# Two scratch rows in turn for VectorE's maxima in a sliding-window attention and GEGLU kernel

## The chip, the core and the metric

The kernel runs on one core of a Trainium2 chip. The metric is the device time of one execution in microseconds; a median of several runs stands for a kernel. A core has five engines that run side by side, each with its own queue of instructions taken in order: TensorE (PE, with a loader for its weights, PEld), VectorE (DVE), ScalarE (ACT), GpSimd (POOL) and SyncE (SP), which here issues most of the transfers. They meet through semaphores: an instruction may wait for a count that another engine, a transfer, or an earlier instruction of its own engine raises.

## The reference

For x of 2048 tokens by 640 features, with xn = layernorm(x):

```python
qkv = xn @ wqkv                          # 32 heads of 20
scores = q @ k.T * 20 ** -0.5            # key in (query - 256, query]
o = softmax(scores) @ v
h = gelu(xn @ w_gate) * (xn @ w_up)      # 1728 wide
out = x + o @ wo + h @ w_down
```

The softmax needs, for each head and query, the largest score in its window of 256 keys, or another value that keeps the exponentials in range.

## The kernel before

The products keep near float32 precision by splitting each operand into a high and a low part. After the layernorm, the main stage is the function `attention`: it goes through 32 units (8 groups of four heads by 4 chunks of 512 queries), each of 14 slots, and writes out by hand the order of TensorE's, ScalarE's, VectorE's, GpSimd's and SyncE's work. A slot can hold maxima, exponentials, the product with the values, and in any case some matmuls of a filler: the projections to q, k and v, and a part of the gate and up products. When the units are done, the rest of the gate and up products and the output products follow, without maxima.

The maxima belong to `max_pair` (L503). One call takes one head from each half of the array's rows and 128 queries. It takes two PSUM banks (`bank("ps_m")`, L510), computes into each of them the scores of 128 queries against 288 keys (L523), and then VectorE reads each bank once (L527): it adds the mask, which is 0 inside the window and −3e38 outside, and takes the maximum along the row. Only that one number per query is of use; it goes to a column of the tile `mx`. The instruction must write the masked sums somewhere too, and that is `junk`, 128 partitions by 288 bfloat16, which nobody reads. In the profile one such maximum is two instructions of VectorE, both on L527: the maximum (`junk<-ps_m,mask`) and the read of its accumulator (`mx<-`).

There are 8 such pairs per unit, pulled from a stream by `pull_max` two at a time: in the slots 0, 4 and 8, and in slot 0 a second time after `av_unit`, the product with the values (L622). So 4 maxima make one burst, and 512 are run in all. When a unit's 16 are done, `negate` (L536, L537) turns them and `max_end` (L541, its matmul is L544) brings them into the rows of the stacked queries, so that the exponential of `exp_piece` (scores L582, ScalarE's exponential L584) already has the maximum subtracted.

All these matmuls write to one ring of six PSUM banks (the pool `psr`, L482): `ps_m`, `ps_o` (two for each product with the values), `ps_e` and `ps_n`. A matmul that starts in a bank waits until the reader of the bank's previous content is done: VectorE for `ps_m`, ScalarE for the others. Which bank of the ring each of them gets isn't written in the kernel: the framework's planner hands out the one that it believes free first. The same planner places every tile and sets every wait. The filler writes to two other banks (`psd`, L132), which VectorE also reads in parts of the projections (L273) and of the gate and up products (L677, L685, L692).

A tile of a pool with `bufs=1` has one place: whoever writes a new tile of that tag waits until all accesses to the old one are over. That holds for an engine's own earlier instructions too: the planner adds a wait on VectorE's own semaphore. Where an instruction needs two waits, the second is an instruction of the engine's sequencer ahead of it (EVENT_SEMAPHORE in the profile, not counted as busy). Here that is the usual case: one wait is for TensorE's scores, one for the maximum before.

Of the kernel before, what the change touches and what calls it, by code (L numbers as in the profile page):

```python
# [11 lines left out]
BF = mybir.dt.bfloat16  # L12
# [58 lines left out]
def block_kernel(ctx, tc, x, wqk, wv, wgu, wdo, wdl, out):  # L71
# [143 lines left out]
    def late(fn, *a):  # L215
        if now[0] is None or now[0] < NS:
            fn(*a)
        else:
            lates.append((fn, a))
# [263 lines left out]
    ap = pr.enter_context(tc.tile_pool(name="ap", bufs=2, side="right", reuse_waits="tile"))  # L483
# [14 lines left out]
    def bank(name):  # L498
        return psr.tile([128, C], F32, name=name, tag="ring")
# [3 lines left out]
    def max_pair(u, i):  # L503
        g, c = divmod(u, NC)
        jj, b = divmod(i, 4)
        q, k = qs[u % NQ], ks[u % NK]
        if i == 0:
            maxes[u] = ap.tile([128, 4, 4], F32, name="mx", tag="mx")
        n = 128 * b + 128 if c == 0 and b < 2 else 288
        pss = [bank("ps_m") for _ in range(2)]  # L510
        todo = []
        for h in range(4):
            q0 = 128 * b + 32 * h
            k0 = q0 + 32 - n
            parts = [(max(0, -k0), n, k, max(0, k0), q0 + 32)]
            if k0 < 0:
                parts.append((0, -k0, ks[(u - 1) % NK], C + k0, C) if c else (0, -k0, k, 0, None))
            todo += [(i_, h, q0, *part) for i_, part in enumerate(sorted(parts, key=lambda p: p[1] - p[0]))]
        for _, h, q0, lo, hi, kt, k0, k1 in sorted(todo, key=lambda p: p[:2]):
            for r, ps in enumerate(pss):  # L520
                rows, j = slice(64 * r, 64 * r + SR), 2 * r + jj
                keys = kt[rows, j, k0:k1] if k1 else kt[rows, j, 0:1].to_broadcast([SR, hi])
                nc.tensor.matmul(ps[32 * h:32 * h + 32, lo:hi], q[rows, j, q0:q0 + 32], keys,  # L523
                                 start=True, stop=True, tile_position=(64 * r, 32 * h))
        junk = ap.tile([128, 288], BF, name="junk", tag="junk", bufs=1)
        for r, ps in enumerate(pss):
            nc.vector.tensor_tensor_reduce(out=junk[:, 0:n], in0=ps[:, 0:n], in1=mask[:, 288 - n:288], scale=1.0,  # L527
                                           scalar=NEG, op0=OP.add, op1=OP.max,
                                           accum_out=maxes[u][:, 2 * r + jj, b:b + 1])
        if i == 7:  # L530
            mx = maxes.pop(u)
            nm = nms[u % 2]
            maxes[u] = nm

            def negate():
                nc.vector.tensor_scalar(nm[:, 0, 0], mx, -1.0, None, op0=OP.mult)  # L536
                nc.vector.scalar_tensor_tensor(nm[:, 0, 1], mx, -1.0, nm[:, 0, 0], op0=OP.mult, op1=OP.subtract)  # L537

            late(negate)
# [262 lines left out]
    def pull_max(n, slot):  # L802
        for _ in range(n):
            x = next(stream, None)
            if x is None:
                return
            max_pair(*x)
            if x[1] == 7:
                at(slot + (MXD if slot >= 0 else 4), max_end, x[0])
# [714 lines left out]
```

## Time and profile before

| | |
|---|---|
| median of 3 runs | 1045.38 us (1043.09 to 1048.82) |
| profiled execution | 1044.52 us |
| its span, first to last instruction | 1042.8 us |
| TensorE busy | 1027.2 us (99%) |
| VectorE busy | 728.3 us (70%) |
| of that the maxima, L527 | 512, 445 ns in the mean, from 62.8 to 540.6 us |
| mean granted clock of TensorE | 0.999 |

The span is what the trace covers; the execution's time has 1.7 us around it. Busy shares are means over stages that differ. Matmuls overlap in the array and their ends are modelled, so TensorE's busy time says that something was under way and not that the array was full: part of a stop can lie under the recorded length of the matmul before it.

### The profile page before, as it was taken

What the parts mean: (1) busy time and instruction counts of PE and PEld (TensorE: products, weight loads), DVE (VectorE), ACT (ScalarE), POOL (GpSimd) and SP (SyncE); (2) the same over time, 40 slices, a digit from 0 to 9 for tenths busy, and PEclk for the clock granted to TensorE, in tenths of its full rate; (3) what the DMA queues carried; (4) which work ended last, traced back from release to release, by engine and by line L of the source; (5) the groups of instructions that cost most, each with busy time, mean ns of one, the idle gap of its engine ahead of it and who ended that gap; (6) DMA issues with size and microseconds to landing.
All of it is one profiled execution on the core that took longest, in us unless ns stands there. A gap on an engine that the chain in (4) does not pass through costs nothing.

```text
span 1042.8 us, 28733 instructions
## 1 busy us (share of the span) xinstructions
PE 1027.2 (99%) x10941; PEld 853.3 (82%) x10941; DVE 728.3 (70%) x2007; ACT 527.8 (51%) x1120; POOL 377.1 (36%) x543
## 2 busy tenths in 40 slices
PE   8999999999999999999999999999999999999998
PEld 7987776677678876777677888888888999999998
DVE  8845666666665566776653778777556879888887
ACT  4444667666666667666666522323234544333332
POOL 5221778876565568665755111110110000000000
PEclk9999999999999999999999999999999999999999
DMA  5652465555333354444332557666216874443342
GB/s 201 190 148 62 134 180 162 171 158 175 104 105 93 94 168 135 150 126 142 100 92 91 190 187 248 232 240 243 102 66 248 257 234 137 136 128 119 119 137 92
DMA packets 105203, 158.95 MB, mean 152 GB/s; under 512 B 15420, under 2 KB 60092, under 8 KB 105064
## 3 DMA queue, kind: packets, MB, share of 16 engines
q1 hardware_dynamic: 102680, 150.95, 45.9%
q10 hardware_dynamic: 2384, 6.16, 1.9%
q8 instruction: 86, 1.41, 0.6%
q14 instruction: 53, 0.43, 0.1%
HBM read 101.78 MB, written 54.92 MB: 150 GB/s over the span
## 4 chain that ended last, share of the span: by engine, by line
PE 84%; DVE 7%; DMA 4%; ACT 2%; issue 1%; SPq 1%; POOL 0%; ACTq 0%; DVEq 0%
PE ps_d L110 22%; PE ps_g L968 21%; PE ps L1235 14%; PE ps_e L582 8%; PE ps_v L110 7%; PE ps_o L622 6%; PE ps_m L523 4%; DVE junk L527 2%; PE ps_g L110 1%; DVE ss L1073 1%; DMA qs<-qd 1%; DVE at L1073 1%; PE ps_t L181 1%; DVE wt L1073 1%; DMA stg<-wtd 1%
## 5 line engine op out<-in xcount | busy, mean ns | idle before, releaser
L527 DVE CUSTOM_DVE_ANT_0 junk<-ps_m,mask 128x288 bf16<-128x288 f32 (+2 forms) x512 | 227.8, 445 | 140.3 <-PE ps_m L523 82.5
L584 ACT ACTIVATE P<-ps_e 128x512 f32<-128x512 f32 (+2 forms) x384 | 195.5, 574 | 60.0 <-PE ps_e L582 58.9
L1235 PE MATMUL ps<-wb,at 128*128 128x320 f32 x999 | 156.4, 310 | 0.8 <-DVE xr L1261 0.7
L1235 PEld LDWEIGHTS ps<-wb,at 128*128 128x128 f32 x999 | 148.9, 188 | 1.4 <-issue 0.9
L595 POOL TENSOR_SCALAR_AFFINE_SELECT P<-P 128x512 f32<-128x512 f32 x128 | 83.8, 656 | 93.5 <-ACT P L584 92.2
L582 PE MATMUL ps_e<-qs,ks 124*128 124x128 bf16 (+2 forms) x704 | 107.3, 277 | 2.1 <-DVE mx L527 2.0
L110 PE MATMUL ps_d<-xh,wql 128*128 128x512 f32 x350 | 105.3, 410 | 0.0
L110 PE MATMUL ps_d<-xl,wqh 128*128 128x512 f32 x350 | 105.3, 410 | 0.0
L110 PE MATMUL ps_d<-xh,wqh 128*128 128x512 f32 x350 | 105.3, 411 | 0.0
L1235 PE MATMUL ps<-wt,at 128*128 128x320 f32 x552 | 89.3, 310 | 0.4 <-DVE u L1073 0.4
L582 PEld LDWEIGHTS <-ks 124*128 124x128 bf16 x704 | 51.5, 98 | 41.0 <-issue 24.0
L1235 PEld LDWEIGHTS ps<-wt,at 128*128 128x128 f32 x552 | 82.9, 188 | 0.9 <-DVE u L1073 0.9
L1189 ACT ACTIVATE at<-ss 128x512 fp32r<-128x512 f32 x59 | 37.3, 633 | 91.4 <-DVE ss L1073 91.4
L622 PE MATMUL ps_o<-P,v 64*32 64x320 f32 (+5 forms) x2816 | 82.0, 348 | 0.0
L103 POOL TENSOR_TENSOR wql<-wr,wqh 128x640 fp32r<-128x640 f32 x11 | 17.6, 1605 | 173.9 <-PE ps_g L968 129.4
L598 POOL TENSOR_SCALAR_AFFINE_SELECT P<-P 128x512 f32<-128x512 f32 x112 | 71.3, 647 | 16.9 <-ACT P L584 16.8
L622 PEld LDWEIGHTS ps_o<-P,v 64*32 64x32 f32 x2816 | 66.7, 106 | 9.8 <-DVE mx L527 4.5
L110 PEld LDWEIGHTS ps_d<-xh,wql 128*128 128x128 f32 x350 | 63.9, 189 | 12.8 <-issue 1.6
L110 PEld LDWEIGHTS ps_d<-xh,wqh 128*128 128x128 f32 x350 | 63.3, 189 | 12.6 <-issue 0.9
L110 PEld LDWEIGHTS ps_d<-xl,wqh 128*128 128x128 f32 x350 | 63.6, 189 | 12.1 <-issue 1.5
L523 PE MATMUL ps_m<-ks,qs 60*32 60x96 bf16 (+5 forms) x3008 | 64.9, 244 | 3.8 <-DVE mx L527 2.3
L259 POOL TENSOR_TENSOR pt<-r,pt 128x512 bf16<-128x512 f32 x40 | 46.8, 1170 | 57.4 <-ACT pt L258 57.4
(196 smaller groups left out, 1889.4 us busy)
## 6 DMA issues: line engine op xcount, KB each, us to landing
hr<-hd SPq DMA_DIRECT2D x104, 128.0 KB
hd<-he SPq DMA_DIRECT2D x50, 256.0 KB
wr<-wgu SPq DMA_DIRECT2D x27, 320.0 KB
qs<-qd SPq DMA_DIRECT2D x64, 120.0 KB
ks<-kd SPq DMA_DIRECT2D x64, 120.0 KB
xi<-x SPq DMA_DIRECT2D x16, 320.0 KB
qs<-qd SPq DMA_DIRECT2D x64, 80.0 KB
ks<-kd SPq DMA_DIRECT2D x64, 80.0 KB
```

What stands on the lines that cost most here:

```text
L110: nc.tensor.matmul(ps, a(k), b(k), start=n == 0, stop=n == 3 * nk - 1)
L259: nc.gpsimd.tensor_tensor(out=pt[:, l, :], in0=r, in1=pt[:, 1, :], op=OP.subtract)
L523: nc.tensor.matmul(ps[32 * h:32 * h + 32, lo:hi], q[rows, j, q0:q0 + 32], keys, start=True, stop=True, tile_position=(64 * r, 32 * h))
L527: nc.vector.tensor_tensor_reduce(out=junk[:, 0:n], in0=ps[:, 0:n], in1=mask[:, 288 - n:288], scale=1.0, scalar=NEG, op0=OP.add, op1=OP.max ...
L582: nc.tensor.matmul(ps[:, col:col + n], k[0:QROWS, j, kc:kc + 128], q[0:QROWS, j, q0:q0 + n], start=True, stop=True)
L584: nc.scalar.activation(pt[:, j, lo:hi], ps[:, lo:hi], AF.Exp, scale=SCALE)
L595: nc.gpsimd.affine_select(out=a, in_=a, pattern=[[0, 4], [1, 128]], compare_op=OP.is_ge, fill=0.0, base=0, channel_multiplier=-1)
L598: nc.gpsimd.affine_select(out=a, in_=a, pattern=[[0, 4], [-1, 128]], compare_op=OP.is_ge, fill=0.0, base=-1, channel_multiplier=1)
L622: nc.tensor.matmul(halves[h][32 * j:32 * j + 32, q0:q0 + n], v[rows, w0_:w0_ + 32], pts[u, bi][rows, j, col:col + n], start=i == 0, stop=i ...
L968: nc.tensor.matmul(ps, i, j, start=first and n == 0, stop=n == len(work) - 1, skip_group_check=True)
L1189: nc.scalar.activation(hi[:, 3:7], s, AF.Copy)
L1235: nc.tensor.matmul(ps[bank][:, 0:HD], *work[bank][j], start=bank not in begun, stop=final[p, bank] == n and j == len(work[bank]) - 1, skip ...
```

## The change

The scratch row is taken inside the loop over the two banks, so that each maximum has a tile of its own, where the two maxima of a pair had one together; and the tag has two places in place of one.

```diff
@@ -522,8 +522,8 @@
                 keys = kt[rows, j, k0:k1] if k1 else kt[rows, j, 0:1].to_broadcast([SR, hi])
                 nc.tensor.matmul(ps[32 * h:32 * h + 32, lo:hi], q[rows, j, q0:q0 + 32], keys,
                                  start=True, stop=True, tile_position=(64 * r, 32 * h))
-        junk = ap.tile([128, 288], BF, name="junk", tag="junk", bufs=1)
         for r, ps in enumerate(pss):
+            junk = ap.tile([128, 288], BF, name="junk", tag="junk", bufs=2)
             nc.vector.tensor_tensor_reduce(out=junk[:, 0:n], in0=ps[:, 0:n], in1=mask[:, 288 - n:288], scale=1.0,
                                            scalar=NEG, op0=OP.add, op1=OP.max,
                                            accum_out=maxes[u][:, 2 * r + jj, b:b + 1])
```

The number of instructions on the engines stays the same in the code; the order written out by hand stays too. The tile takes 576 bytes per partition, once more than before.

## The prediction

> **What bounds the kernel now.** I read the page first: the busy times, then the group of the line that the change touches.
>
> ```profile
> span 1042.8 us, 28733 instructions
> PE 1027.2 (99%) x10941; PEld 853.3 (82%) x10941; DVE 728.3 (70%) x2007; ACT 527.8 (51%) x1120; POOL 377.1 (36%) x543
> L527 DVE CUSTOM_DVE_ANT_0 junk<-ps_m,mask 128x288 bf16<-128x288 f32 (+2 forms) x512 | 227.8, 445 | 140.3 <-PE ps_m L523 82.5
> ```
>
> TensorE (PE) sets the time: of 1042.8 us it is idle 1042.8 − 1027.2 = 15.6. VectorE (DVE) has slack on average, so whatever a faster maximum saves there counts only where TensorE waits for a maximum. The view of the line itself gives where the maxima lie, and that nearly all of them have a wait of their own ahead of them.
>
> ```profile
> L527 DVE CUSTOM_DVE_ANT_0 junk<-ps_m,mask x512: 278/458/460, 62.8 to 540.2; 128x288 bf16<-128x288 f32 x149, 128x128 bf16<-128x128 f32 x11, 128x256 bf16<-128x256 f32 x11
> L527 DVE DVE_READ_ACCUMULATOR2_ANT mx<- x512: 76/83/86, 63.0 to 540.6; 128x1 f32 x171
> ```
>
> ```profile
> L527 DVEq EVENT_SEMAPHORE  x469: 21/21/21, 63.2 to 540.1; - x157
> ```
>
> So only the stretch from 62.8 to 540.6 us, the attention, can change; what follows has no maxima. Each maximum is two instructions: the masked maximum (0.46 us) and the read of its accumulator (0.08 us), and 469 of 512 have a sequencer wait in front. Next come the waits for the maxima, in the stretch from 60 to 560 us: engine and line, who released it, total us, times, longest.
>
> ```profile
> PE ps_m L523 <- DVE mx L527: 2.3, 7, 0.3
> PE ps_e L582 <- DVE mx L527: 2.0, 6, 0.5
> PEld ps_o L622 <- DVE mx L527: 4.5, 9, 0.5
> PEld L544 <- DVE mx L527: 3.2, 12, 0.3
> ```
>
> These four are the whole field of the change: matmuls that need a bank of the six-bank ring which a maximum still reads. The first two are idle time of TensorE itself, 4.3 us; the others are idle time of its weight loader, beside which TensorE may be working. Last, the chain of waits over the same 500 us:
>
> ```profile
> by line: PE ps_d L110 42.2%; PE ps_e L582 16.4%; PE ps_o L622 11.3%; PE ps_v L110 10.5%; PE ps_m L523 8.3%; DVE junk L527 3.4%; DMA qs<-qd 2.5%; issue 1.4%; SPq L494 0.8%; SPq L268 0.5%; ACT P L584 0.5%; PE ps_n L544 0.4%; DVE nm L536 0.3%;
> ```
>
> The maxima hold 3.4% of it, 17 us. That isn't what a faster maximum could give back, since TensorE works beside most of it, but it serves as a check below.
>
> **The change, part by part.** No instruction is removed and none added: 512 maxima, 512 accumulator reads. What moves is the row that the masked sums are written to. Where all write one row, each maximum must wait until the one before it has written; with two rows in turn it needs the one before that. In the program before, 432 of the 512 wait for the maximum directly in front of them. One burst shows what that costs, both engines together:
>
> ```profile
> 181.53 0.81 PE L523 MATMUL ps_m<-ks,qs 60*32 60x288 bf16 x6
> 181.54 0.46 DVE L527 CUSTOM_DVE_ANT_0 junk<-ps_m,mask 128x288 bf16<-128x288 f32 x1
> 181.93 0.08 DVE L527 DVE_READ_ACCUMULATOR2_ANT mx<- 128x1 f32 x1
> ...
> 182.16 0.46 DVE L527 CUSTOM_DVE_ANT_0 junk<-ps_m,mask 128x288 bf16<-128x288 f32 x1
> ...
> 182.54 0.08 DVE L527 DVE_READ_ACCUMULATOR2_ANT mx<- 128x1 f32 x1
> 182.68 0.31 PE L523 MATMUL ps_m<-ks,qs 60*32 60x288 bf16 x7 [0.33 <-DVE mx L527]
> ...
> 182.77 0.46 DVE L527 CUSTOM_DVE_ANT_0 junk<-ps_m,mask 128x288 bf16<-128x288 f32 x1
> ```
>
> The period is 0.61 us (181.54, 182.16, 182.77): the accumulator read starts 0.38 after the maximum, overlapping its end, is done at 0.47, and then nothing runs for 0.14 us until the next maximum starts. An instruction that has nothing to wait for behaves otherwise:
>
> ```profile
> 414.38 0.46 DVE L527 CUSTOM_DVE_ANT_0 junk<-ps_m,mask 128x288 bf16<-128x288 f32 x1
> 414.77 0.09 DVE L527 DVE_READ_ACCUMULATOR2_ANT mx<- 128x1 f32 x1
> 414.77 0.69 DVE L273 TENSOR_TENSOR r<-ps_d,pt 128x512 f32<-128x512 f32 x1
> ```
>
> ```profile
> 175.30 0.69 DVE L273 TENSOR_TENSOR r<-ps_d,pt 128x512 f32<-128x512 f32 x1 [1.62 <-POOL pt L259]
> 175.90 0.45 DVE L527 CUSTOM_DVE_ANT_0 junk<-ps_m,mask 128x288 bf16<-128x288 f32 x1
> ```
>
> The subtraction at 414.77 starts together with the accumulator read, 0.39 after the maximum. The maximum at 175.90 starts 0.09 before the recorded end of the instruction ahead of it; it has its wait for an earlier maximum too, one that was long over, so a wait already met costs nothing. What the trace doesn't show is a maximum straight behind another without the wait. The bounds: 0.47, if it must let the accumulator read finish (gain 0.14 each), and 0.38, if it overlaps as the subtraction does (gain 0.23). A loss has no row: the wait can only be met earlier. I take 0.38, the row nearest in kind, and keep 0.14 for the range.
>
> The Trainium skill, page "VectorE: DVE Perf Modes", section "The DRAIN you can't avoid", speaks against any gain: the next VectorE instruction doesn't issue until the pipeline is empty, and a semaphore between two costs nothing extra. By it the period stays at 0.61 and the sum is 0. The rows at 414.77 and 175.90 disagree, with starts 0.08 and 0.09 us ahead of the recorded ends; the section behind it on that page, on two instructions with no wait between them, allows such an early start. I go by the rows.
>
> Over the 432 that is 432 × 0.14 to 0.23 = 60 to 99 us of VectorE time, nearly all hidden under TensorE's 99%. What lies on the path are the four waits.
>
> **ps_m at L523, 7 waits, 2.3 us.** In the burst above TensorE's last matmul before the stop started at about 182.06 (the row's end, 182.34, less its 0.28) and the next at 182.68, 0.62 later, while in an unhindered burst they follow at 0.1 or less. So the real stop is about 0.5, not the 0.33 shown, because a matmul's recorded length covers the start of it: 7 × 0.5 = 3.5 us. These waits come at the second pair of a slot whose four earlier maxima still drain; the fourth has three self-waits behind it, so it comes 3 × 0.14 = 0.42 to 3 × 0.23 = 0.69 earlier. Gain 7 × 0.42 = 2.9 to the whole 3.5.
>
> **ps_e at L582, 6 waits, 2.0 us.** One of them, with its maxima:
>
> ```profile
> 171.40 0.44 DVE L527 CUSTOM_DVE_ANT_0 junk<-ps_m,mask 128x288 bf16<-128x288 f32 x1
> ...
> 171.99 0.46 DVE L527 CUSTOM_DVE_ANT_0 junk<-ps_m,mask 128x288 bf16<-128x288 f32 x1
> ...
> 172.51 0.60 PE L582 MATMUL ps_e<-qs,ks 124*128 124x256 bf16 x4 [0.39 <-DVE mx L527]
> ```
>
> The release is the end of the maximum at 171.99, the second of its burst (the first is at 171.40). One self-wait lies ahead: 0.14 to 0.23 off each, 6 × that = 0.8 to 1.4 us.
>
> **ps_o at L622, 9 waits, 4.5 us.** Always the same picture:
>
> ```profile
> 475.65 0.46 DVE L527 CUSTOM_DVE_ANT_0 junk<-ps_m,mask 128x288 bf16<-128x288 f32 x1 [0.28 <-PE ps_m L523]
> ...
> 476.17 0.45 PEld L622 LDWEIGHTS ps_o<-P,v 64*32 64x32 f32 x25 [0.53 <-DVE mx L527]
> ```
>
> It is the first maximum of a burst that releases it, and that one waited for its matmuls, not for a row. Gain 0.
>
> **L544, 12 waits, 3.2 us.** The loader is idle, TensorE isn't:
>
> ```profile
> 467.81 1.08 PE L110 MATMUL ps_d<-xl,wqh 128*128 128x512 f32 x4
> 468.73 0.23 PE L544 MATMUL ps_n<-identb,nm 128*128 128x128 bf16 x1
> ```
>
> Four projection matmuls from 467.81 to 468.73 are 0.23 each, the next starts on time. Gain 0.
>
> Behind the maxima in VectorE's queue stand the negations (L536) and the projections' parts (L273, L677, L685, L692); they come earlier too, but no row shows TensorE waiting for them in this stretch. The second row takes 576 bytes more per partition, for which the pool of the attention's tiles begins lower; that has no time.
>
> The sum: 2.9 + 0.8 = 3.7 to 3.5 + 1.4 = 4.9 us; with the overlapping start that I chose, 4.9. The check: the chain's 17 us of maxima shrunk by 0.14/0.61 to 0.23/0.61 would be 3.9 to 6.4. The profiled execution took 1044.52 us (span 1042.8 and 1.7 around it), so 1039.6 on its scale; the median of the runs, 1045.38, is 0.86 above it. **Forecast: 1045.4 − 4.9 = 1040.5 us**, 0.47% faster. A measurement of this kernel can tell about 0.5%, 5.2 us, from no change, so this lies just at that edge.
>
> **The rivals.**
>
> *Nothing moves: 1045.4.* A maximum behind a maximum keeps its 0.61, because both use the same accumulator or VectorE empties itself between any two instructions; or the planner doesn't hand out the two rows in turn, or TensorE, arriving earlier, stands as long for another bank. For it: no row has two maxima without the wait, and ScalarE's exponentials share the ring. Against it: the rows at 414.77 and 175.90; the other two-deep tiles of the pool are handed out strictly in turn in the program before; TensorE's waits in this stretch name only maxima and a transfer. The emptying is the rule of the Trainium skill's page "VectorE: DVE Perf Modes" weighed above.
>
> *Faster than the sum: 1036.* The ring's banks are handed out by when the planner believes them free. With quicker maxima it may hand them out otherwise, and if the 9 ps_o waits went with it, 4.5 us more would come off: 1045.4 − 4.9 − 4.5 = 1036.0. Against it: the loader's 0.53 isn't all TensorE's.
>
> *Slower: 1051.5.* The same planner, the other way. In 9 of the 31 units that use the full ring (the 9 waits above) the second half of ps_o gets the bank of the burst's first maximum, since the planner took that for free before the exponential's bank. Quicker maxima look free still sooner, so the other 22 units could get such a bank too, at 4.5/9 = 0.50 us each: +11.0 − 4.9 = +6.1, 1051.5. It decides from 4.9/0.5 = 10 more such units on. For it: the choice is already that close in 9 units. Against it: the first maximum of a burst has no self-wait, so its own planned end moves only where VectorE was behind before.
>
> **How the numbers follow.** The forecast 0.60, nothing moves 0.17, faster than the sum 0.12, slower 0.11. Of the forecast's cases somewhat over half should come out beyond 0.5%, as the check's upper end is 6.4 and the sum's lower end 3.7: 0.33, with the 0.12 that makes faster 0.45. The slower rival passes 0.5% in about 0.08; the rest, 0.47, is the same. The likeliest case's own range is 1039 (6.4 off) to 1041.7 (3.7 off). The range 1036 to 1047 takes in nothing moving, with 1.6 us for the scatter of the runs, and the faster rival's time; it leaves out the slower rival's end.
>
> **What would show it.** In the changed kernel's trace, maxima in a burst start 0.38 to 0.47 us apart instead of 0.61, the read of the accumulator at 0.38 as before. The waits of ps_m for maxima go nearly to nothing, those of ps_e lose a third or more, those of ps_o stay at nine or so of 0.5 us. The maxima's share of the chain falls to some 2%. It is wrong if the period stays at 0.61 (the price), if it falls and TensorE's idle time in 60 to 560 us doesn't (the path), or if the number of ps_o waits changes much (the ring's order).

## The result, and the profile after

The changed kernel takes 1037.63 us in the median of 6 runs (1036.36 to 1038.76), beside 1045.39 us for the kernel before in the same comparison: a ratio of 0.9923, 95% interval 0.9905 to 0.9942. That is 7.8 us less where 4.9 were forecast; 1037.6 lies inside the range of 1036 to 1047, and it is faster by more than the 0.5% that can be told from no change. A second comparison on another chip gave 0.9942 (0.992 to 0.9963), 5.7 us, also clear of no change, though the upper end of its interval is a gain of only 0.37%. The profiled execution took 1036.36 us.

The page of the changed kernel first: its span, the busy times of the engines, and the group of the maxima (busy time, mean ns of one, then the idle time ahead of them and what ended most of it).

```profile
span 1034.6 us, 28689 instructions
PE 1024.6 (99%) x10941; PEld 853.5 (82%) x10941; DVE 711.0 (69%) x2007; ACT 527.5 (51%) x1120; POOL 379.4 (37%) x543
L527 DVE CUSTOM_DVE_ANT_0 junk<-ps_m,mask 128x288 bf16<-128x288 f32 (+2 forms) x512 | 197.6, 441 | 131.4 <-PE ps_m L523 130.8
```

The instructions of the engines are as many as before; 43 of the 44 that the span has fewer are waits of the sequencer ahead of maxima. A maximum takes as long as it did (441 ns against 445); the busy time of the group falls by 30 us because maxima now overlap, and VectorE waits longer for scores (130.8 us against 82.5). A burst in the timeline of the changed kernel (start, length, engine, line) shows how:

```profile
223.09 0.46 DVE L527 CUSTOM_DVE_ANT_0 junk<-ps_m,mask 128x288 bf16<-128x288 f32 x1 [2.49 <-PE ps_m L523]
223.47 0.08 DVE L527 DVE_READ_ACCUMULATOR2_ANT mx<- 128x1 f32 x1
223.47 0.45 DVE L527 CUSTOM_DVE_ANT_0 junk<-ps_m,mask 128x288 bf16<-128x288 f32 x1
...
223.85 0.45 DVE L527 CUSTOM_DVE_ANT_0 junk<-ps_m,mask 128x288 bf16<-128x288 f32 x1
```

The next maximum starts together with the read of the accumulator, 0.38 us after the one ahead of it, where the period before was 0.61. Next the view of the line and the waits of the changed kernel between 60 and 560 us (engine and tile, who released it, total us, times, longest).

```profile
L527 DVEq EVENT_SEMAPHORE  x426: 21/21/21, 63.2 to 532.5; - x142
```

```profile
PE ps_e L582 <- DVE mx L527: 1.1, 3, 0.5
PE ps_m L523 <- DVE r L273: 0.9, 1, 0.9
PE ps_m L523 <- DMA qs<-qd: 0.6, 1, 0.6
...
PEld L544 <- DVE mx L527: 5.1, 19, 0.3
PEld ps_o L622 <- DVE mx L527: 4.5, 9, 0.5
```

The row of ps_m waiting for maxima (2.3 us, 7 times) is gone, ps_e's has fallen from 6 waits to 3, and ps_o's is the same to the digit. New is a wait of ps_m for L273, VectorE's part of a projection. The maxima still wait ahead in the sequencer (426 times, 469 before), but for the maximum before the last. The chain of waits, of which the maxima held 3.4% before, can be followed back in this profile only to 158 us. That of the changed kernel's second profile (run after_again) covers the whole stretch from 60 to 560 us, and there the maxima hold 0.2%:

```profile
by line: PE ps_d L110 45.2%; PE ps_e L582 16.9%; PE ps_o L622 14.6%; PE ps_v L110 10.5%; PE ps_m L523 9.0%; DMA qs<-qd 2.1%; issue 0.6%; PE ps_n L544 0.5%; SPq L494 0.4%; DVE junk L527 0.2%; DVE mx L527 0.0%
```

To see where the time went, each matmul of the trace after was matched with the same matmul of the trace before, and the change of its distance from the start of the matmul ahead of it was put down to the tile it writes. The middle column is the profiled execution above, the last one that of the second comparison:

| where | change, us | second |
|---|---|---|
| ps_m, 8 places at which it had stopped for a maximum | −4.5 | −4.5 |
| ps_m, once behind L273 | +1.0 | 0 |
| ps_m, waits for transfers | −0.6 | +1.8 |
| ps_e, where it had stopped for a maximum | −2.6 | −2.5 |
| ps_e, once behind L273 | +0.6 | +0.7 |
| ps_n, ps_d and ps_o together | −0.5 | −0.5 |
| first ps_g behind the attention | −0.8 | −0.8 |
| after 600 us, output products | −1.2 | +0.2 |
| sum | −8.6 | −5.6 |

The spans differ by 8.2 and 5.5 us; the rest lies at the ends and in two stretches ahead of the attention that cancel (−1.4 and +1.4 us in the first). What both executions have in common is −4.5 − 2.6 + 0.7 − 0.5 − 0.8 = −7.7 us. The other rows, transfers, the single wait behind L273 and the wait for `xr` (L1261) late in the kernel, come and go between two executions of one kernel, by 1 to 2.4 us each, and they make the difference between the two profiles; that they also make the one between the medians of the two comparisons isn't shown. One stop of ps_m for a transfer, 0.6 us at 201.81 in the kernel before, is gone in both executions, but it is gone in e2 too, which has the waits of the kernel before, so it isn't the change's. Whether TensorE, being earlier, meets a late transfer more often wasn't settled; two profiles are too few for it.

### The profile page after: what moved, and what is told of

It reads as the page before. It is cut to its first block, busy times and chain, and to the rows that moved or that the text cites. A ratio compares the mean times of both kernels' runs of the same rounds, so it can differ in the third digit from the quotient of the medians.

```text
span 1034.6 us, 28689 instructions
## 1 busy us (share of the span) xinstructions
PE 1024.6 (99%) x10941; PEld 853.5 (82%) x10941; DVE 711.0 (69%) x2007; ACT 527.5 (51%) x1120; POOL 379.4 (37%) x543
## 4 chain that ended last, share of the span: by engine, by line
PE 81%; DVE 1%; DMA 1%; POOL 1%; SPq 0%; ACT 0%; issue 0%; DVEq 0%
PE ps_g L968 21%; PE ps L1235 21%; PE ps_d L110 17%; PE ps_e L582 7%; PE ps_o L622 6%; PE ps_v L110 3%; PE ps_m L523 3%; PE ps_g L110 1%; DVE ss L1073 0%; DVE at L1073 0%; DMA qs<-qd 0%; SPq L494 0%; ACT at L1189 0%; POOL pt L259 0%; DMA hr<-hd 0%
## 5 line engine op out<-in xcount | busy, mean ns | idle before, releaser
L527 DVE CUSTOM_DVE_ANT_0 junk<-ps_m,mask 128x288 bf16<-128x288 f32 (+2 forms) x512 | 197.6, 441 | 131.4 <-PE ps_m L523 130.8
L582 PE MATMUL ps_e<-qs,ks 124*128 124x128 bf16 (+2 forms) x704 | 106.7, 277 | 1.2 <-DVE mx L527 1.1
L582 PEld LDWEIGHTS <-ks 124*128 124x128 bf16 x704 | 51.5, 98 | 39.4 <-issue 22.5
L622 PE MATMUL ps_o<-P,v 64*32 64x320 f32 (+5 forms) x2816 | 82.0, 348 | 0.0
L622 PEld LDWEIGHTS ps_o<-P,v 64*32 64x32 f32 x2816 | 67.1, 106 | 9.4 <-DVE mx L527 4.5
L523 PE MATMUL ps_m<-ks,qs 60*32 60x96 bf16 (+4 forms) x3008 | 62.9, 244 | 1.6 <-DVE r L273 0.9
```

The costliest lines, as they stand in the source:

```text
L582: nc.tensor.matmul(ps[:, col:col + n], k[0:QROWS, j, kc:kc + 128], q[0:QROWS, j, q0:q0 + n], start=True, stop=True)
L622: nc.tensor.matmul(halves[h][32 * j:32 * j + 32, q0:q0 + n], v[rows, w0_:w0_ + 32], pts[u, bi][rows, j, col:col + n], start=i == 0, stop=i ...
```

## The experiments

The theory is the one of the prediction: the time between two maxima sets when the last banks of a burst come free, and TensorE stops for these. It has rivals. One says that the wait on the row itself matters, whatever the time between maxima (D in the expectations); one that the gain comes from another order of the banks, since the planner hands them out by what it believes of the maxima's ends. In the program of the changed kernel 48 of the ring's 992 tiles, 47 of them ps_m, indeed follow the last use of their bank at another distance than before.

### Half of the change, and the part without effect

e1_pair_rows takes two places, but one row for each pair, so that only the second pair's first maximum is freed. e2_one_row_inner takes a row for each maximum, but one place.

```diff
 e1_pair_rows
-        junk = ap.tile([128, 288], BF, name="junk", tag="junk", bufs=1)
+        junk = ap.tile([128, 288], BF, name="junk", tag="junk", bufs=2)
 e2_one_row_inner
-        junk = ap.tile([128, 288], BF, name="junk", tag="junk", bufs=1)
         for r, ps in enumerate(pss):
+            junk = ap.tile([128, 288], BF, name="junk", tag="junk", bufs=1)
```

> The two maxima of a pair share one row again, and the pairs take two rows in turn: of the three steps in a burst of four maxima only the middle one loses its wait. The banks of the ring are handed out exactly as in the kernel before. Theory A (the gain is the shorter wait between maxima, as far as TensorE waits for them): starts in a burst 0.61, 0.38, 0.61 us apart; the fourth maximum comes 0.23 us earlier instead of 0.69, the second not at all, so 8 waits of ps_m times 0.23 = 1.8 us: about 1043.5. Rival B (more than half of the 7.8 us is the planner's other order of the banks): that order is absent here, so 1045.4 less a few tenths. Rival C (what counts is that two rows are written, not the wait): the whole gain, 1037.6.

> A tile for each maximum as in the changed kernel, but one row for all: every maximum waits for the one before. Bank order as in the kernel before. Theory A: period 0.61 us, time 1045.4, no difference that can be measured. Rival C': the tile of its own for each maximum has a share in the gain: below 1043.

e2 made no difference: 1043.92 us, 1.0002 (0.9988 to 1.0016), with the waits of before. e1 took 1040.26 us, 0.9964 (0.9952 to 0.9976), against 1044.16 us for the kernel before on the same chip: 3.9 us less, where 1.8 had been expected. Its maxima in the timeline stand 0.61, 0.38 and 0.61 apart:

```profile
224.53 0.46 DVE L527 CUSTOM_DVE_ANT_0 junk<-ps_m,mask 128x288 bf16<-128x288 f32 x1 [2.03 <-PE ps_m L523]
...
225.14 0.46 DVE L527 CUSTOM_DVE_ANT_0 junk<-ps_m,mask 128x288 bf16<-128x288 f32 x1
...
225.52 0.45 DVE L527 CUSTOM_DVE_ANT_0 junk<-ps_m,mask 128x288 bf16<-128x288 f32 x1
...
226.13 0.46 DVE L527 CUSTOM_DVE_ANT_0 junk<-ps_m,mask 128x288 bf16<-128x288 f32 x1
```

One step of 0.23 us saved per burst of four, and TensorE's stop behind it shrinks by as much. The same burst of scores in three timelines, kernel before, changed kernel, e1, from the second pair's scores (ps_m) to the filler's next matmul (ps_d):

```profile
227.19 0.31 PE L523 MATMUL ps_m<-ks,qs 60*32 60x288 bf16 x4
...
227.95 0.31 PE L523 MATMUL ps_m<-ks,qs 60*32 60x288 bf16 x7 [0.33 <-DVE mx L527]
...
228.19 1.20 PE L110 MATMUL ps_d<-xh,wqh 128*128 128x512 f32 x4
```

```profile
224.68 0.31 PE L523 MATMUL ps_m<-ks,qs 60*32 60x288 bf16 x4
...
225.15 0.72 PE L110 MATMUL ps_d<-xh,wqh 128*128 128x512 f32 x2
```

```profile
226.12 0.31 PE L523 MATMUL ps_m<-ks,qs 60*32 60x288 bf16 x3
...
226.89 0.50 PE L110 MATMUL ps_d<-xh,wqh 128*128 128x512 f32 x1
```

1.00 us before, 0.47 with two rows, 0.77 with e1. By the matching of matmuls e1's eight places of ps_m give 2.0 us of the 4.5, about what was expected; what surprised is 1.2 us at ps_e, for which the prediction had seen one self-wait ahead. The section on why comes back to it. e1's program hands out the banks exactly as the program before, and so no other order of banks is needed for a gain.

### The order of the banks held fixed

To take the planner out, the ring is handed out in strict rotation, six tags with one place each, without the change (e8_rotate_one_row) and with it (e7_rotate_two_rows).

```diff
-    psr = pp.enter_context(tc.tile_pool(name="psr", bufs=6, space=PSUM, reuse_waits="tile"))
+    psr = pp.enter_context(tc.tile_pool(name="psr", bufs=1, space=PSUM, reuse_waits="tile"))
...
+    taken = [0]
...
-        return psr.tile([128, C], F32, name=name, tag="ring")
+        taken[0] += 1
+        return psr.tile([128, C], F32, name=name, tag=f"ring{taken[0] % 6}")
```

> The changed kernel, with the six banks of the ring handed out strictly in rotation instead of by the planner: the 9 units in which ps_o waits for the burst's first maximum are gone. Theory A: the ps_o waits vanish (4.5 us of the loader, about 0.2 us of TensorE each, 1.8 us), other waits appear where the planner had left the rotation for cause (three units around a late bank): 1036 to 1038. With the one-row kernel in the same rotation it shows the period's worth at one and the same bank order: by theory A 5 to 7 us between the two; by rival B (order of the banks makes more than half) at most 4.

> The kernel before, with the six banks strictly in rotation; bank order the same as in the two-row kernel in rotation. Theory A: 5 to 7 us slower than that one, 1042 to 1044, maxima 0.61 us apart, the waits of ps_m for maxima there as in the kernel before. Rival B: 1038 to 1040, since the order of the banks carries most of the gain.

e8 took 1042.65 us, 0.9988 (0.9975 to 1.0002), so the rotation alone gives nothing that can be told. e7 took 1032.72 us, 0.9888 (0.9871 to 0.9906), 3 us below what was expected. With one and the same order of banks, the second row is worth 1042.65 − 1032.72 = 9.9 us, more than the 5 to 7 expected; between the two traces ps_e gives 5.0 us of it and ps_m 4.2. The waits of e8, then of e7, 60 to 560 us (rotation moves the lines on by 3):

```profile
PE ps_e L585 <- DVE mx L530: 4.2, 16, 0.4
PE ps_m L526 <- DVE mx L530: 2.5, 8, 0.3
...
```

```profile
PE ps_e L585 <- DVE mx L530: 1.6, 2, 1.3
PE ps_m L526 <- DVE r L273: 0.5, 1, 0.5
PE ps_o L625 <- POOL P L601: 0.2, 1, 0.2
```

The nine ps_o waits for a burst's first maximum are in neither. Their worth by the matching of matmuls is 4.7 us, from the kernel before to e8 as from the changed kernel to e7: 0.5 to 0.65 us at each of eight places, nothing at the ninth, where ps_o now waits for GpSimd. With one row all of it comes back at ps_e (+4.9 us, 16 waits), since ps_e now gets banks whose maxima are late; with two rows 4.3 us stay in the attention (−4.2 for all of ps_o, −2.0 at ps_m, where part is transfers that come and go, and +1.9 at ps_e).

### The time between maxima, or the wait

All further kernels have the rotated banks, so that they compare with e7 and e8. e4_half_one_row keeps the one row and its wait, but its maxima read half of the columns; e5_half_two_rows does the same with two rows. Both leave half of the keys out of the maximum. e9_in_place writes the masked sums back to the scores' own bank and has no scratch row at all.

```diff
 e4_half_one_row (e5_half_two_rows: with the change besides)
-            nc.vector.tensor_tensor_reduce(out=junk[:, 0:n], in0=ps[:, 0:n], in1=mask[:, 288 - n:288], scale=1.0,
+            m = n // 2
+            nc.vector.tensor_tensor_reduce(out=junk[:, m:n], in0=ps[:, m:n], in1=mask[:, 288 - m:288], scale=1.0,
 e9_in_place
-        junk = ap.tile([128, 288], BF, name="junk", tag="junk", bufs=1)
...
-            nc.vector.tensor_tensor_reduce(out=junk[:, 0:n], in0=ps[:, 0:n], in1=mask[:, 288 - n:288], scale=1.0,
+            nc.vector.tensor_tensor_reduce(out=ps[:, 0:n], in0=ps[:, 0:n], in1=mask[:, 288 - n:288], scale=1.0,
```

> One row, banks in rotation, each maximum over the later half of its columns alone (144 of 288), so it leaves out half of the keys of the maximum. The wait for the row stays; the maximum is about 0.15 us shorter, the spacing about 0.46 us. Theory A: the two kernels in rotation give 9.9 us for 0.23 us of spacing; 0.15 of it are 6.5 us: 1036. A first maximum of a burst also ends 0.15 earlier. Rival D: the wait is still there, so 1041 to 1042.6.

> Two rows, banks in rotation, half the columns per maximum (leaves out half of the keys of the maximum): spacing about 0.23 us. Theory A: with 0.38 us most stops of TensorE for a maximum are gone already, so little is left: 1031 to 1032.5. If the gain went on in proportion, 0.15 us more would be 6.5 us: 1026.

> Banks in rotation; the masked sums are written back into the bank that they were read from, so that there is no scratch row and no wait of a maximum for another at all. Theory A: a wait that is met already costs nothing, so the same as two rows in rotation, 1032.7 within 0.2%, if the write to the bank is as quick as that to the row; maxima 0.38 us apart. Rival: the write into PSUM is slower, a maximum takes 0.5 us and more, 1035 to 1042.

Two maxima of e4 in the timeline, half as wide and 0.47 us apart here (0.46 in the median), each still with its wait:

```profile
300.64 0.31 DVE L531 CUSTOM_DVE_ANT_0 junk<-ps_m,mask 128x144 bf16<-128x144 f32 x1
...
301.11 0.31 DVE L531 CUSTOM_DVE_ANT_0 junk<-ps_m,mask 128x144 bf16<-128x144 f32 x1
```

And what its matmuls wait for:

```profile
PE ps_m L526 <- DMA qs<-qd: 0.7, 1, 0.7
PE ps_e L586 <- DVE mx L531: 0.5, 2, 0.3
...
```

With the wait kept and the time between maxima shortened, the gain is there, more of it than the 1036 us expected, and the waits of ps_m for maxima are gone. So the rival of the wait falls. One order of banks, with the median time from one maximum's start to the next:

| kernel | apart, us | median, us | ratio (95%) |
|---|---|---|---|
| e8, one row | 0.61 | 1042.65 | 0.9988 (0.9975 to 1.0002) |
| e4, one row, half the columns | 0.46 | 1033.48 | 0.9883 (0.9857 to 0.9909) |
| e9, in place | 0.42 | 1034.29 | 0.9889 (0.9864 to 0.9914) |
| e7, two rows | 0.38 | 1032.72 | 0.9888 (0.9871 to 0.9906) |
| e5, two rows, half the columns | 0.23 | 1032.33 | 0.9875 (0.9846 to 0.9905) |

The ratios of the first and the fourth are to 1044.16 us for the kernel before, those of the others to 1045.81 us on another chip. Nothing is gained below about 0.46 that can be told: what is left in the lists of e4, e9 and e7 are two or three stops of TensorE for a maximum, 0.5 to 1.7 us in all, and each of these maxima stood in VectorE's queue behind an L273 that had waited for GpSimd or ScalarE. In e8, e4 and e7 the fourth maximum of a burst ends 2.29, 1.69 and 1.59 us behind the first one's start, so what counts lies between the first two of these; in e4 the first maximum ends 0.15 us earlier too, and its share isn't told apart from that of the time between maxima. In e9 a maximum takes 0.50 us in place of 0.46 and its accumulator read 0.14 us in place of 0.08, as its rival had it, but the maxima start 0.38 to 0.42 us apart, and the time is that of two rows.

The opposite was tried too: two rows, with the time to the next maximum brought back to 0.61. e6_fill_two_rows puts two small additions behind each maximum, e10_max_and_half a second maximum over half of the columns into a spare column. Both add work that nobody uses.

```diff
 e6_fill_two_rows, behind the maximum
+            for o in (0, 46):
+                nc.vector.tensor_tensor(out=one[:, o:o + 46], in0=mask[:, 0:46], in1=mask[:, 46:92], op=OP.add)
 e10_max_and_half, behind the maximum
+            m = n // 2
+            again = ap.tile([128, 288], BF, name="junk", tag="junk", bufs=2)
+            nc.vector.tensor_tensor_reduce(out=again[:, 0:m], in0=ps[:, 0:m], in1=mask[:, 288 - m:288], scale=1.0,
+                                           scalar=NEG, op0=OP.add, op1=OP.max,
+                                           accum_out=spare[:, 2 * r + jj, b:b + 1])
```

> Two rows, banks in rotation, and behind each maximum two small VectorE additions (128x46, into a tile that nobody reads) that fill about 0.25 us: no maximum waits for another, but they start about 0.63 us apart as with one row. Theory A (the spacing of the maxima is what TensorE feels, whatever makes it): back to the one-row kernel in rotation or a little above, 1042 to 1046. Rival D (VectorE waiting for itself is what costs, a delay that other work would hide): stays near 1032.7, at most 1035.

> Two rows, banks in rotation, and behind each maximum a second one over half of the columns of the same bank, into a spare tile (more work, none left out): no maximum waits for the row just written, but whole maxima start about 0.38 + 0.23 = 0.61 us apart, as with one row, and the bank is free about when it was there. Theory A (spacing): as the one-row kernel in rotation, 1042 to 1045, the more since the burst's first bank also comes free 0.23 later. Rival D (it is VectorE's wait for itself that costs): near 1032.7.

e6 took 1148.31 us, 1.0984 (1.0955 to 1.1013), and tells nothing of the question: its filling isn't of one length. A pair of additions takes 0.31 us without a running GpSimd instruction; beside one it takes 0.75 us here, 0.86 in the median and up to 2.6:

```profile
300.18 0.75 DVE L534 TENSOR_TENSOR one<-mask 128x46 f32<-128x46 f32 x2
300.20 0.67 POOL L600 TENSOR_SCALAR_AFFINE_SELECT P<-P 128x512 f32<-128x512 f32 x1
...
303.06 0.45 DVE L530 CUSTOM_DVE_ANT_0 junk<-ps_m,mask 128x288 bf16<-128x288 f32 x1
...
303.44 0.31 DVE L534 TENSOR_TENSOR one<-mask 128x46 f32<-128x46 f32 x2
```

e10 has the steady 0.61 us that was wanted, with no wait for the maximum in front:

```profile
301.65 0.45 DVE L533 CUSTOM_DVE_ANT_0 junk<-ps_m,mask 128x288 bf16<-128x288 f32 x1
...
302.03 0.30 DVE L538 CUSTOM_DVE_ANT_0 junk<-ps_m,mask 128x144 bf16<-128x144 f32 x1
...
302.26 0.46 DVE L533 CUSTOM_DVE_ANT_0 junk<-ps_m,mask 128x288 bf16<-128x288 f32 x1
```

```profile
PE ps_e L593 <- DVE spare L538: 4.6, 18, 0.4
PE ps_m L527 <- DVE spare L538: 3.0, 10, 0.3
```

It took 1055.97 us, 1.011 (1.0074 to 1.0146), slower than was expected of either theory. TensorE's waits are back, nearly as in e8 (4.2 and 2.5 us), without the wait on the row: that again speaks for the time at which the banks come free. The excess has one cause that the waits show: each bank is released by the second, half maximum and so about 0.23 us later than in e8. The matmuls of the two traces, matched, put most of it there: of 10.8 us between them, 8.5 are 39 groups of ps_m and ps_e matmuls that take 0.16 to 0.25 us longer each, and 1.6 are a single wait of ps_m for a transfer.

### Both again, side by side

> The changed kernel once more, for its scatter and beside the rotated one on the same chip: 1037.6, ratio 0.992 to 0.994. The steps that theory A puts down to the maxima stand where they stood; if what was gained at the transfers of qs and behind 800 us (1.7 us together in the first pair of traces) is scatter, it differs here.

> Two rows with the banks in rotation, beside the changed kernel on the same chip: 1032.7, 0.4 to 0.5% below it.

The changed kernel took 1038.31 us, 0.9942 (0.992 to 0.9963), the rotated version with two rows 1033.98 us, 0.9903 (0.9881 to 0.9924), with 1043.97 us for the kernel before. The version of e7 beats both kernels, by 4.3 us the changed one: each of its six runs is below each of the changed kernel's six. It needs the second row for that, as e8 shows.

## Why the prediction was right, and where its sizes were off

*The price.* 0.38 us was chosen over 0.47, by the row of the subtraction that starts beside the accumulator read; the burst at 223.09 shows 0.38. The Trainium skill, page "VectorE: DVE Perf Modes", section "The DRAIN you can't avoid", has the semaphore between two VectorE instructions cost nothing extra, as measured there on a chain of copies; by the trace it cost 0.61 − 0.38 = 0.23 us per maximum here, and the rival that nothing moves has fallen with it.

*ps_m at L523.* The mechanism was right, the term undersized: 2.9 to 3.5 us forecast, 4.5 measured in both profiles. The seven listed stops gave 3.5 us, 0.5 each, as forecast. Three more, at 182.06, 242.82 and 449.26 us, gave 1.0 us though they aren't in the list of waits: TensorE's idle time there shows as 0.01 to 0.14 us, as the stop lay under the recorded length of the matmul ahead. The step that failed is the count of 7 taken from that list.

*ps_e at L582.* Here a step was wrong: "One self-wait lies ahead". The maximum that released ps_e at 172.51 was the second of its burst, but VectorE had been late for a whole burst by then. The timeline of the kernel before, from the burst ahead of it, shows no idle time in between but the 0.14 us that each self-wait leaves:

```profile
166.65 0.46 DVE L527 CUSTOM_DVE_ANT_0 junk<-ps_m,mask 128x288 bf16<-128x288 f32 x1 [0.37 <-PE ps_m L523]
...
168.48 0.46 DVE L527 CUSTOM_DVE_ANT_0 junk<-ps_m,mask 128x288 bf16<-128x288 f32 x1
...
168.98 1.21 DVE L536 TENSOR_SCALAR nm<-mx 128x16 bf16<-128x16 f32 x1
170.22 0.65 DVE L537 SCALAR_TENSOR_TENSOR nm<-mx,nm 128x16 bf16<-128x16 f32 x1
170.80 0.68 DVE L273 TENSOR_TENSOR r<-ps_d,pt 128x512 f32<-128x512 f32 x1
```

Four self-waits, 4 × 0.23 = 0.92 us, lie ahead of the release and go together, so the stops vanish whole, 0.54 us at 172.51 and again at 279.69, instead of shrinking by 0.14 to 0.23. Two of the six listed, at 96.22 and 99.67, gained nothing, as the first maximum of a burst released them. The 0.8 to 1.4 us forecast measured 2.6; e1's unexpected 1.2 us at ps_e is the same thing.

*What was given back.* The prediction saw no wait of TensorE for what stands behind the maxima. There is one with what stands ahead of them: L273 waits for GpSimd, and the maxima wait behind it in VectorE's queue. In the changed kernel:

```profile
175.00 0.69 DVE L273 TENSOR_TENSOR r<-ps_d,pt 128x512 f32<-128x512 f32 x1 [3.01 <-POOL pt L259]
...
175.61 0.45 DVE L527 CUSTOM_DVE_ANT_0 junk<-ps_m,mask 128x288 bf16<-128x288 f32 x1
...
176.12 0.60 PE L582 MATMUL ps_e<-qs,ks 124*128 124x128 bf16 x4 [0.48 <-DVE mx L527]
```

VectorE idles 3.01 us, the first maximum behind is late, and ps_e stops for it: 0.6 us of the gain, in both profiles. The list of waits puts this one down to the maximum; it goes back to GpSimd, which L273 waited for.

*ps_o at L622, and L544.* Gain 0 for both was right: nine waits of ps_o, 4.5 us, as before, and 0.0 us at these places by the matching. L544's waits rose from 3.2 to 5.1 us of the loader's time and cost nothing. But that the loader's 0.53 "isn't all TensorE's" was wrong: e7 and e8 show 0.5 to 0.65 us of TensorE's time at eight of the nine places.

*The planner.* The slower rival fell, since the count of ps_o waits didn't change. The faster one was right that the order of the banks would change, and wrong as to where it tells: not in the nine waits but at the end of the attention. There the first ps_g matmul of the kernel before waits for ScalarE's copy out of a ps_o bank (L627), and the changed kernel's doesn't:

```profile
566.06 0.73 PE L110 MATMUL ps_g<-xh,wqh 128*128 128x512 f32 x2 [0.51 <-ACT P L627]
```

```profile
558.85 1.32 PE L110 MATMUL ps_g<-xh,wqh 128*128 128x512 f32 x5
558.88 0.59 ACT L627 ACTIVATE P<-ps_o 128x512 f32<-128x512 f32 x1
```

The matmul starts beside the copy instead of behind it: 0.8 us that no step of the prediction had. e1, whose banks are as before, doesn't have this gain.

*The check.* The chain's 17 us times the share by which the period fell, 3.9 to 6.4 us, came nearer than the sum; the sign that it gave, a share of some 2%, was too cautious, as the maxima fell to 0.2%. Added up, the forecast of 4.9 stands against 4.5 + 2.6 − 0.7 + 0.5 + 0.8 = 7.7 us in the traces and 5.7 to 7.8 us between medians. The range holds with some luck: 1037.6 lies below the likeliest case's own 1039 to 1041.7, and inside the whole range only because that reached down to the faster rival's 1036, whose mechanism, the ps_o waits going, didn't come about.

## What to carry to other kernels

A scratch tile that nobody reads still orders the instructions that write it: look for a sequencer wait on the engine's own last instruction, and price it by a pair of neighbours that has no such wait. Count the stops by the starts of the matmuls, since a list of waits leaves out those that a recorded length covers, check each against a second run, since waits for transfers come and go, and follow the engine that releases a bank back to where it last idled, as all waits since then count. Where a planner hands out a ring of banks by its own idea of when they are free, strict rotation is one edit worth a try: here it was worth nothing that can be told with one scratch row and some 4 us with two.

## What the runs showed of the hardware beside

The negation L536, 128 by 16 from SBUF to SBUF, has a duration that depends on GpSimd. The view of the line, kernel before and changed kernel (ns: shortest, median, longest):

```profile
L536 DVE TENSOR_SCALAR nm<-mx x32: 174/448/1206, 77.7 to 540.7; 128x16 bf16<-128x16 f32 x32
```

```profile
L536 DVE TENSOR_SCALAR nm<-mx x32: 174/714/1198, 77.1 to 533.2; 128x16 bf16<-128x16 f32 x32
```

Of the 64 negations (L536 and L537) 26 have no GpSimd instruction beside them in the kernel before, and these take about 0.175 us; the other 38 take 0.50 us in the median and up to 1.2. In the changed kernel 55 of 64 meet one, which is why the median rises though the instruction is the same. Of these 93 in the two traces, 92 end 0.03 to 0.04 us behind the end of a GpSimd instruction. One of them, from its timeline:

```profile
400.49 1.28 POOL L628 TENSOR_TENSOR ob<-ob,P 128x512 f32<-128x512 f32 x1
...
400.99 0.81 DVE L536 TENSOR_SCALAR nm<-mx 128x16 bf16<-128x16 f32 x1
```

401.77 for the one, 401.80 for the other. The maxima, with one operand in PSUM, keep their 0.45 us throughout. The Trainium skill, page "SBUF — State Buffer", section "SBUF: two separate sides", has VectorE and GpSimd share a port pair as an exclusive lock, and the rows agree with a lock: the negation's end follows GpSimd's. e6's additions, two operands in SBUF, show the same stretching: the 512 pairs took 309 us in all, where 512 of 0.31 us would be 159. How much of e6's 10% is due to this wasn't told apart.
